# Attention output of batches 2 to 7 by plain float32 matmuls in the array's quadrants, and the tokens' scales through DRAM

## The chip, the cores and the metric

The kernel runs on one core of a Trainium2 chip. The metric is the device time of one execution in microseconds, the median of several. A core has a matrix engine (TensorE, in the profile PE for matmuls and PEld for the loads of their weights), three engines for elementwise work (VectorE or DVE, ScalarE or ACT, GpSimd or POOL), and SyncE (SP), whose queue issues all the DMAs of this kernel in program order. TensorE reads SBUF and writes PSUM, which has eight banks of 512 float32 in each of 128 partitions. Each engine does its own instructions in order and waits on semaphores for the others.

## The reference

For each of 8 batches and 8 heads, with 576 tokens and 64 features, linear attention without a softmax, a normalisation of each token within its head, and then a feed-forward layer over all 4608 tokens:

```python
kv = np.einsum('bhsd,bhse->bhde', k, v)
out = np.einsum('bhsd,bhde->bhse', q, kv)
rms = np.sqrt(np.mean(out * out, axis=-1, keepdims=True) + 1e-06)
x = out / rms * g_norm          # heads side by side: 4608 x 512
h = x @ w_in                    # 512 x 2048
y = (h / (1 + np.exp(-h))) @ w_out   # 2048 x 512
```

Everything is float32. The weights arrive as 64-bit words and are decoded in the kernel.

## The kernel before

**The feed-forward layer** is the bulk. The 4608 tokens are nine tiles of 512 (`TN`), each tile 16 steps (`NF`), one for every 128 columns of `w_in`. Operands are split into two float32r parts, upper and lower, and three products of the parts make up one product at nearly full precision. Tiles 0 and 1 are done plainly (`products`, `gate`, `project`). Tiles 2 to 4 take two steps at a time in `pair_step`, tiles 5 to 8 in `seven_step`; both use seven products for eight, and load sums of blocks of the weights from DRAM (`load_sums`, L666) twice in each pair of steps.

**The attention** of the batches that follow is threaded into these steps. `plan(b, g)` puts each piece of work of batch `b` into one of three lists, `first_jobs`, `mid_jobs` and `last_jobs`, under the number of a step; the step's code runs the lists at its beginning, in its middle and at its end. `real` maps the plan's steps to the tiles' steps, leaving out the last two of each of the tiles 0 to 4. Batches 2 to 7 start at the plan's steps 14, 23, 32, 41, 51 and 60 (`AT`), so their work lies in the tiles 0 to 5. The order is by hand (`manual_schedule`), and a tile of a pool that is full waits for the last use of the oldest one.

One batch is four pairs of heads (class `Pair`), with the features of two heads on the 128 partitions. In the order of time for batches 2 to 7:

- `load` (L266): k and v of a pair, later q, into tiles of the pool `kvq` (8 tiles), by SP.
- `kv_block` (L1240): the kv matrices of all pairs into one PSUM bank, by plain float32 matmuls in the array's left and right column halves (L277); `copy_kv` copies them on ScalarE into the two diagonal blocks of `kvm`, whose other blocks are zero.
- `split_q`, `low_q` (L299, L302) and `split_kv`, `low_kv` (L290, L293): the upper parts by ScalarE, the lower ones by VectorE. `qh` and `ql` are two more tiles of `kvq`.
- `out_half`, twice a pair: three float32r matmuls of the whole array over 256 or 320 tokens (`mm_out`, L314 to L316), then `copy_out` (L320, L321): the square and a copy out of the bank by ScalarE. The first half stands in the middle of a step, the second at its end. The banks of the attention are one PSUM bank at first and two from tile 1 on (`at_bank`).
- `turn_sq`, `sum_turned` (L325, L328): VectorE turns 32 x 32 blocks of the squares and sums them, which leaves each token's sum on the partitions of its block; four copies between partitions and `rsqrt` then make the scales by Newton steps.
- `spread` (L339): VectorE turns the scales back so that each token's scale stands on all the partitions of its head (`yT`), and `scale` (L347) multiplies `o` by it and by `g_norm`.
- `keep` (L354): SP stores the result in DRAM (`x_in_dram`), from where the later tiles load it.

The pool `tmp` has five tiles, which serve `sq`, `sqT` and `yT` here, the output rows `ob` at the end of tiles, and sums of blocks.

Of the kernel before, what the change touches and what calls it, by code (L numbers as in the profile page):

```python
# [8 lines left out]
F32 = mybir.dt.float32  # L9
# [26 lines left out]
def linear_attention_rms_silu_ffn(  # L36
# [27 lines left out]
    TN = 512  # L64
    NT = B * S // TN
    CUT = 256
    LAG = 2
    WARM = 2
    OUT7 = 5
# [184 lines left out]
    class Pair:  # L254


        def __init__(self, b, c):
            self.b, self.c = b, c
            self.kvm = kvm[c]

        def load(self, place=None, which="kvq"):


            for name in which:
                t = place() if place else kvq.tile([P, S], F32, name=name, tag="kvq")
                nc.sync.dma_start(out=t, in_={"k": k, "v": v, "q": q}[name][self.b, self.c])  # L266
                setattr(self, name, t if name == "q" else t.rearrange("p (r d) -> p r d", d=D))
# [42 lines left out]
        def mm_out(self, half):  # L310

            self.w = w = (slice(0, CUT), slice(CUT, S))[half]
            self.ps = ps = at_bank()[:, :w.stop - w.start]
            nc.tensor.matmul(out=ps, lhsT=self.kh, rhs=self.ql[:, w], start=True, stop=False)  # L314
            nc.tensor.matmul(out=ps, lhsT=self.kl, rhs=self.qh[:, w], start=False, stop=False)  # L315
            nc.tensor.matmul(out=ps, lhsT=self.kh, rhs=self.qh[:, w], start=False, stop=True)  # L316
# [27 lines left out]
        def scale(self, segment):  # L344
            a, e, t, o = (0, S, 3, 0) if segment is None else segments(self.b)[segment]
            to = x32(self.c, slice(o, o + e - a)) if t == 2 else self.o[:, a:e]
            nc.vector.scalar_tensor_tensor(  # L347
                out=to, in0=self.o[:, a:e], scalar=gcol, in1=self.yT, op0=ALU.mult, op1=ALU.mult
            )

        def keep(self):
# [4 lines left out]
        def to_tile(self, segment):  # L356
            a, e, t, o = segments(self.b)[segment]
            th, tl = (x_part(t, i, self.c)[:, o:o + e - a] for i in range(2))
            nc.scalar.copy(out=th, in_=self.o[:, a:e])
            nc.gpsimd.tensor_tensor(out=tl, in0=self.o[:, a:e], in1=th.bitcast(F32), op=ALU.subtract)  # L360

    class FirstPair(Pair):

# [101 lines left out]
    def rsqrt(sums, y, on_tensor):  # L465

        n = NP * (S // 32)
        sums, y = (t.rearrange("p c j -> p (c j)") for t in (sums, y))
        if on_tensor:
            bank = at_bank()  # L470
            m, u = bank[:, 0:n], bank[:, n:2 * n]
            nc.tensor.matmul(out=m, lhsT=both, rhs=sums, start=True, stop=True)
            calls = [lambda: nc.vector.tensor_scalar(
                out=m, in0=m, scalar1=float(D) * EPS, scalar2=None, op0=ALU.add
            )]
        else:
# [13 lines left out]
        return calls + 3 * newton(y, u, m)  # L490
# [81 lines left out]
    HF, H = NF // 2, TN // 2  # L572
    low, high = slice(0, H), slice(H, TN)
    sums_in_dram = dram.tile([HF, 2, P, 2, 2 * H], F32, name="sums_in_dram")
    out_sums = dram.tile([HF, 2, P, 2, 2 * H], F32, name="out_sums")
    operands, x_sums, once, homes, ahead = {}, {}, {}, {}, {}

# [624 lines left out]
    def at_third(n, *calls):  # L1202
        at((first_jobs, mid_jobs, last_jobs)[n % 3], n // 3, *calls)
# [12 lines left out]
    def plan(b, g):  # L1216

        ps = [Pair(b, c) for c in range(NP)]
        norms = []

        def real(g):
            if b == 1:
                return g
            if g < NF - 2:
                return g + 2
            end = OUT7 * (NF - 2)
            return g // (NF - 2) * NF + g % (NF - 2) if g < end else OUT7 * NF + 2 * (g - end)
# [12 lines left out]
        def kv_block():  # L1240

            bank = at_bank()
            for p in ps:
                p.mm_kv(bank[:, p.c * D:(p.c + 1) * D], range(4), start=p.c == 0)
            for p in ps:
                p.mm_kv(chunks=[4], stop=p.c == NP - 1)
            banks.append(bank)

        def copy_kv():

            bank = banks.pop()[:, :NP * D].rearrange("p (c d) -> p c d", d=D)
            for h in range(2):
                d = slice(h * D, (h + 1) * D)
                nc.scalar.copy(out=all_kvm[d, :, d], in_=bank[d])

        banks = []
        if b > 1:
            for p, jobs, i in zip(ps, (last_jobs, first_jobs, first_jobs, first_jobs), (-6, -5, -4, -3)):
                at(jobs, g + i, lambda p=p: p.load(which="kv"))
            at(last_jobs, g - 2, kv_block)  # L1260
            for p in ps:
                at(first_jobs, g - 1 + p.c // 3 * 2, lambda p=p: p.load(which="q"))
            at(first_jobs, g - 1, copy_kv)
        else:
            at(last_jobs, g, kv_block)
            for p in ps:
                at(first_jobs, g + 1, p.copy_kv)
        for p in ps:
            half = [lambda p=p, i=i: out_half(p, i) for i in range(2)]
            sums = lambda p=p: p.sum_sq(norms[0][:, p.c])  # L1270
            if b == 1:
                split_at, first_at, second_at, sums_at, _ = SECOND[p.c]
                at_third(split_at, p.split_kv, p.low_kv, p.split_q, p.low_q)
                at_third(first_at, p.begin_out, half[0])
                at_third(second_at, half[1])
                at_third(sums_at, *[begin] * (p.c == 0), sums)
                continue
# [7 lines left out]
            at(last_jobs, s + 3, *[begin] * (p.c == 0), lambda p=p: p.sum_turned(norms[0][:, p.c]))  # L1285
        s = g + 7
        if b == 1:
            at(chains, 12, lambda: rsqrt(*norms, True))
        else:
            calls = []  # L1290

            def some(count):
                if not calls:
                    calls.extend(rsqrt(*norms, False))
# [286 lines left out]
```

## Time and profile before

| | |
|---|---|
| Median of three runs | 804.53 us |
| The three runs | 802.23, 804.53, 806.88 us |
| Profiled execution, first to last instruction (span) | 802.5 us |
| Matmuls of `out` for batches 1 to 7 (L314 to L316), first and last start | 53 to 454 us |
| Mean granted TensorE clock | 0.997 |
| Moved by DMA | 171.08 MB, 213 GB/s |

The profile was taken of one execution. It gives its span and no separate device time. Busy times of engines are shares of the span; an engine that is not the one that sets the end may idle at no cost. A matmul's end is modelled, so the distance between starts of matmuls says what one costs, not its recorded duration. Rows of the timeline give start and duration in microseconds, engine, line, operation, what is written and read, and shape; in brackets stands the idle time of the engine before and what ended it.

### The profile page before, as it was taken

The page shows a single profiled execution, that of the slowest core. Times are in us where ns is not written, and L with a number is a line of the kernel's source. Part 1 is how long each engine was busy: PE and PEld are TensorE (multiplying, and loading weights), DVE is VectorE, ACT ScalarE, POOL GpSimd, SP SyncE. Part 2 cuts the span into 40 slices and gives each one's busy share as a digit, 9 for nine tenths or more (in the row PEclk, how much of TensorE's full clock was granted, in tenths as well). Part 3 has the DMA queues.
Part 4 walks back from the last instruction along what each step waited for, and adds up shares of the span by engine and source line. Part 5 has one row for each costly group of instructions (what it writes and reads, how often), then busy time and mean ns, then how long its engine had stood idle before and what let it go on. Part 6 is the DMA issues. An engine that isn't in the chain of part 4 may idle for free.

```text
span 802.5 us, 18480 instructions
## 1 busy us (share of the span) xinstructions
PE 788.8 (98%) x7292; PEld 782.4 (97%) x7292; DVE 611.3 (76%) x1328; ACT 413.8 (52%) x871; POOL 112.4 (14%) x116
## 2 busy tenths in 40 slices
PE   8999999999999999999999999999999999999997
PEld 7899999999999999999999999999999999999997
DVE  5999956699779678668778677678867886788666
ACT  4887555445445445535645545335644654455443
POOL 2799781332000000000000000000000000000000
PEclk9999999999999999999999999999999999999999
DMA  9994012744666856676667536986677577667653
GB/s 347 412 413 142 1 61 91 238 150 161 224 212 219 302 185 216 212 262 208 212 234 241 170 101 211 313 267 221 210 242 230 198 226 258 209 203 224 197 187 117
DMA packets 86745, 171.08 MB, mean 213 GB/s; under 512 B 8322, under 2 KB 47746, under 8 KB 86658
## 3 DMA queue, kind: packets, MB, share of 16 engines
q1 hardware_dynamic: 86658, 169.90, 62.3%
q8 instruction: 57, 0.93, 0.5%
q14 instruction: 30, 0.25, 0.1%
HBM read 137.36 MB, written 32.51 MB: 212 GB/s over the span
## 4 chain that ended last, share of the span: by engine, by line
PE 89%; DVE 3%; POOL 2%; issue 2%; ACT 2%; DMA 1%; DVEq 0%; POOLq 0%; ACTq 0%
PE hp L737 32%; PE acc L511 24%; PE acc L913 10%; PE hp L511 9%; PE at L913 5%; PE hp L913 3%; PE at L277 2%; PE at L314 1%; POOL wo L216 1%; PE at L315 1%; PE at L316 1%; DMA wi<-sums_in_dram 1%; PE hp L1340 1%; DMA out<-ob 1%; DVE x_second L729 0%
## 5 line engine op out<-in xcount | busy, mean ns | idle before, releaser
L511 PE MATMUL acc<-wo,gh 128*128 128x256 f32 x1280 | 200.8, 277 | 0.3 <-POOL wo L216 0.3
L511 PEld LDWEIGHTS acc<-wo,gh 128*128 128x128 f32 x1280 | 171.2, 188 | 0.6 <-POOL wo L216 0.5
L737 PE MATMUL hp<-x_second,wi 128*128 128x256 f32 x1152 | 154.2, 278 | 2.6 <-ACT gf L800 2.6
L737 PEld LDWEIGHTS hp<-x_second,wi 128*128 128x128 f32 x1152 | 141.9, 189 | 3.0 <-ACT gf L800 2.9
L511 PE MATMUL acc<-wo,gl 128*128 128x256 f32 x640 | 124.9, 276 | 0.0
L737 PE MATMUL hp<-operand,wi 128*128 128x256 f32 x912 | 121.1, 277 | 0.6 <-DMA wi<-sums_in_dram 0.3
L737 PEld LDWEIGHTS hp<-operand,wi 128*128 128x128 f32 x912 | 111.3, 188 | 1.2 <-DMA wi<-sums_in_dram 0.5
L511 PEld LDWEIGHTS acc<-wo,gl 128*128 128x128 f32 x640 | 96.6, 188 | 0.0
L859 ACT ACTIVATE wi<-wi 128x512 f32<-128x512 f32 x64 | 40.5, 633 | 97.7 <-DVE wi L1161 72.3
L964 POOL TENSOR_TENSOR e<-e,partial 128x256 f32<-128x256 f32 x2 | 1.5, 732 | 597.1 <-DVE e L964 597.1
L913 PE MATMUL acc<-wo,gh 128*128 128x256 f32 x256 | 46.8, 276 | 0.0
L511 PE MATMUL hp<-x_second,wi 128*128 128x256 f32 x384 | 46.3, 277 | 0.0
L511 PE MATMUL hp<-x,wi 128*128 128x256 f32 x360 | 44.5, 278 | 0.8 <-POOL x L462 0.8
L511 PEld LDWEIGHTS hp<-x_second,wi 128*128 128x128 f32 x384 | 45.0, 188 | 0.1
L511 PEld LDWEIGHTS hp<-x,wi 128*128 128x128 f32 x360 | 42.4, 188 | 1.2 <-POOL x L462 1.0
L320 ACT ACTIVATE sq<-at 128x256 f32<-128x256 f32 (+1 forms) x56 | 23.0, 411 | 39.6 <-PE at L316 31.9
L913 PE MATMUL acc<-s,gs 128*128 128x256 f32 x288 | 42.9, 276 | 0.0
L1161 DVE TENSOR_TENSOR wi<-hp,partial 128x256 f32<-128x256 f32 x32 | 13.6, 425 | 35.9 <-PE hp L737 35.9
L913 PEld LDWEIGHTS acc<-wo,gh 128*128 128x128 f32 x256 | 38.6, 188 | 0.0
L913 PEld LDWEIGHTS acc<-s,gs 128*128 128x128 f32 x288 | 37.3, 188 | 0.0
L1146 ACT COPY wi<-hp 128x256 f32<-128x256 f32 x32 | 11.9, 373 | 48.8 <-PE hp L737 48.8
L737 PE MATMUL hp<-moved,wi 128*128 128x256 f32 x288 | 36.6, 276 | 0.0
(207 smaller groups left out, 1660.1 us busy)
## 6 DMA issues: line engine op xcount, KB each, us to landing
wi<-sums_in_dram SPq DMA_DIRECT2D x112, 512.0 KB, 3.7
s<-out_sums SPq DMA_DIRECT2D x96, 256.0 KB, 4.5
wi<-in_moe_w_in SPq DMA_DIRECT2D x16, 512.0 KB, 8.1
wo<-in_moe_w_out SPq DMA_DIRECT2D x16, 512.0 KB, 9.0
sums_in_dram<-sum_parts SPq DMA_DIRECT2D x16, 512.0 KB, 2.9
out_sums<-wi SPq DMA_DIRECT2D x16, 512.0 KB, 3.0
k<-in_k SPq DMA_DIRECT2D x28, 288.0 KB, 4.6
v<-in_v SPq DMA_DIRECT2D x28, 288.0 KB, 5.1
```

Source lines behind the costliest of these rows:

```text
L216: nc.gpsimd.tensor_tensor(out=w[:, 1, :], in0=full, in1=w[:, 0, :].bitcast(F32), op=ALU.subtract)
L277: nc.tensor.matmul(out=self.kv[h], lhsT=self.k[rows, c, :], rhs=self.v[rows, c, :], start=(start and r == 0), stop=(stop and r == 4),)
L314: nc.tensor.matmul(out=ps, lhsT=self.kh, rhs=self.ql[:, w], start=True, stop=False)
L315: nc.tensor.matmul(out=ps, lhsT=self.kl, rhs=self.qh[:, w], start=False, stop=False)
L316: nc.tensor.matmul(out=ps, lhsT=self.kh, rhs=self.qh[:, w], start=False, stop=True)
L320: nc.scalar.activation(out=self.sq[:, self.w], in_=self.ps, func=AF.Square)
L511: nc.tensor.matmul(out=to[:, at:at + 256], lhsT=stationary, rhs=moving[:, at:at + 256], start=start and at == 0, stop=stop and at == n - 256,)
L737: nc.tensor.matmul(out=out, lhsT=a_of(i, a, c), rhs=x[b][:, c], start=start and n == 0, stop=n == 5, skip_group_check=not check,)
L859: nc.scalar.activation(out=self.gated, in_=self.gated, func=AF.Silu)
L913: nc.tensor.matmul(out=self.out[m], lhsT=g[m], rhs=self.weight(m, j, a), start=j == 0 and n == 0 and m in self.opens, stop=j == HF - 1 and ...
L1146: nc.scalar.copy(out=first.gated[:, low], in_=u)
L1161: nc.vector.tensor_tensor(out=first.gated[:, high], in0=u, in1=u3, op=ALU.add)
```

## The change

For batches 2 to 7:

- Four heads are one group. The host lays out q so that one tile holds, for 288 of the 576 tokens (`HS`), two heads on the upper and two on the lower 64 partitions, side by side; the heads in k and v are reordered to match. Two such tiles (`half` 0 and 1) cover a group, so a batch has four jobs (class `Job`).
- A job's `mm_out` does four plain float32 matmuls, one for each head: the stationary operand is the head's 64 x 64 kv matrix, the moving one its 64 x 288 q. A head with its features on the lower partitions and its output on the upper ones, and so on, takes each of the four quadrants. The two row halves write two PSUM banks. The upper and lower parts of q and kv, and their eight instructions per pair, are gone; kv is copied once as it is.
- The whole job, matmuls and copies out, stands at the end of a step; `turn_sq` and `sum_turned` stay where they were.
- The Newton steps stand two thirds of a step earlier. VectorE turns the scales once for the batch (`turn_scales`), SP stores them in a small buffer in DRAM (two stores), and later loads each pair's row back, repeated over the 64 partitions of each head (`load_scales`: two loads for each pair, a step ahead of `scale`). `yT` lies in `kvq`, for batch 7 in `tmp`. `scale` of batch 2 moves from the middle to the end of its step.

```diff
+    class Job:
+        def __init__(self, b, n, chunks):
+            self.b, self.n = b, n
+            self.u, self.half = divmod(n, 2)
+            self.chunks = chunks
+            self.w = slice(self.half * HS, (self.half + 1) * HS)
+
+        def load(self):
+            self.q = kvq.tile([P, S], F32, name="q", tag="kvq")
+            nc.sync.dma_start(out=self.q, in_=q[self.b, self.n])
+
+        def mm_out(self, kv):
+            self.banks = [at_bank()[:, :HS] for _ in range(2)]
+            for i, r in ((0, 0), (1, 1), (1, 0), (0, 1)):
+                rows, to = (slice(x * D, (x + 1) * D) for x in (r, i))
+                nc.tensor.matmul(
+                    out=self.banks[r][to], lhsT=kv[rows, 2 * self.u + i], rhs=self.q[rows, i * HS:(i + 1) * HS],
+                    start=True, stop=True,
+                )
+
+        def copy_out(self):
+            self.sq = tmp.tile([P, S], F32, name="sq", tag="tmp")
+            for i, (bank, chunk) in enumerate(zip(self.banks, self.chunks)):
+                if not self.half:
+                    chunk.o = opool.tile([P, S], F32, name="o")
+                nc.scalar.activation(out=self.sq[:, i * HS:(i + 1) * HS], in_=bank, func=AF.Square)
+                nc.scalar.copy(out=chunk.o[:, self.w], in_=bank)
...
         def begin():
-            norms[:] = [small.tile([P, NP, S // 32], F32, name=name) for name in ("sums", "y")]
+            sums = small.tile([P, NP, S // 32], F32, name="sums")
+            scales = small.tile([P, ROWS], F32, name="y")
+            norms[:] = sums, scales[:, :NP * (S // 32)].rearrange("p (c j) -> p c j", c=NP), scales
+            nc.gpsimd.memset(scales[:, NP * (S // 32):], 0.0)
+
+        def turn_scales():
+            turned = const.tile([P, P], F32, name="turned", tag="kh", bufs=2)[:, :ROWS]
+            nc.vector.transpose(out=turned, in_=norms[2])
+            for h in range(2):
+                nc.sync.dma_start(
+                    out=scales_in_dram[b % 2, h].rearrange("(j m) a -> m j a", m=32),
+                    in_=turned[h * D:h * D + 32].rearrange("m (j a) -> m j a", a=32),
+                )
+
+        def load_scales(p):
+            p.yT = kvq.tile([P, S], F32, name="yT", tag="kvq") if b + 1 < B else tmp.tile([P, S], F32, name="yT", tag="tmp")
+            n = S // 32
+            for h in range(2):
+                row = scales_in_dram[b % 2, h, p.c * n:(p.c + 1) * n].rearrange("(o j) a -> o (j a)", o=1)
+                nc.sync.dma_start(out=p.yT[h * D:(h + 1) * D], in_=row.to_broadcast([D, S]))
...
-            s = g + p.c
-            at(mid_jobs, s, p.split_q)
-            at(last_jobs, s, p.low_q, p.split_kv)
-            at(first_jobs, s + 1, p.low_kv)
-            at(mid_jobs, s + 2, p.begin_out, half[0])
-            at(last_jobs, s + 2, half[1])
-            at(mid_jobs, s + 3, p.turn_sq)
+            for f in fours:
+                s = g + f.n
+                at(last_jobs, s + 2, lambda f=f: f.mm_out(kv[0]), f.copy_out)
+                at(mid_jobs, s + 3, f.turn_sq)
+                at(last_jobs, s + 3, *[begin] * (f.n == 0), lambda f=f: f.sum_turned(norms[0]))
...
             for n, count in enumerate((6, 3, 3, 3)):
-                at((first_jobs, mid_jobs, last_jobs)[(2 + n) % 3], s + (2 + n) // 3, lambda count=count: some(count))
+                at((first_jobs, mid_jobs, last_jobs)[n % 3], s + n // 3, lambda count=count: some(count))
+            at(first_jobs, s + 1, turn_scales)
 
         def x_stages(p, s, *parts):
+            if b > 1:
+                at(last_jobs, s - 1, lambda: load_scales(p))
             for part in parts:
-                at(mid_jobs, s, lambda part=part: p.spread(norms[1][:, p.c], part))
-                at(mid_jobs if b <= 2 else last_jobs, s, lambda part=part: p.scale(part))
+                if b == 1:
+                    at(mid_jobs, s, lambda part=part: p.spread(norms[1][:, p.c], part))
+                at(mid_jobs if b == 1 else last_jobs, s, lambda part=part: p.scale(part))
             if b > 1:
                 at(first_jobs, s + 1, p.keep)
```

More of the change, by code (lines that the diff above doesn't have):

```diff
@@ L347, in scale @@
             nc.vector.scalar_tensor_tensor(
-                out=to, in0=self.o[:, a:e], scalar=gcol, in1=self.yT, op0=ALU.mult, op1=ALU.mult
+                out=to, in0=self.o[:, a:e], scalar=gcol, in1=self.yT[:, a:e] if self.b > 1 else self.yT,
+                op0=ALU.mult, op1=ALU.mult,
             )
@@ L360, in to_tile, with turn_sq, sum_turned @@
             nc.gpsimd.tensor_tensor(out=tl, in0=self.o[:, a:e], in1=th.bitcast(F32), op=ALU.subtract)
+    class Job:
[22 more added lines that the diff above has]
+                nc.scalar.copy(out=chunk.o[:, self.w], in_=bank)
+        def turn_sq(self):
+            self.sqT = tmp.tile([P, S], F32, name="sqT", tag="tmp")
+            nc.vector.transpose(out=self.sqT, in_=self.sq)
+        def sum_turned(self, sums):
+            blocks = HS // 32
+            nc.vector.tensor_reduce(
+                out=sums[:, 2 * self.u:2 * self.u + 2, self.half * blocks:(self.half + 1) * blocks],
+                in_=self.sqT.rearrange("p (c j a) -> p c j a", c=2, a=32), axis=AX.X, op=ALU.add,
+            )
     class FirstPair(Pair):
@@ L574, in linear_attention_rms_silu_ffn @@
     sums_in_dram = dram.tile([HF, 2, P, 2, 2 * H], F32, name="sums_in_dram")
+    scales_in_dram = dram.tile([2, 2, ROWS, 32], F32, name="scales_in_dram")
     out_sums = dram.tile([HF, 2, P, 2, 2 * H], F32, name="out_sums")
@@ L1249, in copy_kv @@
         def copy_kv():
[L1251 to L1256, printed above, removed]
+            kv.append(const.tile([P, NP, D], F32, name="kv_all", tag="kvm"))
+            nc.scalar.copy(out=kv[0], in_=banks.pop()[:, :NP * D].rearrange("p (c d) -> p c d", d=D))
+        banks, kv = [], []
         if b > 1:
+            fours = [Job(b, n, ps[n // 2 * 2:n // 2 * 2 + 2]) for n in range(NP)]
             for p, jobs, i in zip(ps, (last_jobs, first_jobs, first_jobs, first_jobs), (-6, -5, -4, -3)):
@@ L1260, in plan @@
             at(last_jobs, g - 2, kv_block)
-            for p in ps:
-                at(first_jobs, g - 1 + p.c // 3 * 2, lambda p=p: p.load(which="q"))
+            for f in fours:
+                at(first_jobs, g - 1 + f.n // 3 * 2, f.load)
             at(first_jobs, g - 1, copy_kv)
+            for f in fours:
+                s = g + f.n
+                at(last_jobs, s + 2, lambda f=f: f.mm_out(kv[0]), f.copy_out)
+                at(mid_jobs, s + 3, f.turn_sq)
+                at(last_jobs, s + 3, *[begin] * (f.n == 0), lambda f=f: f.sum_turned(norms[0]))
         else:
@@ L1267, in plan @@
                 at(first_jobs, g + 1, p.copy_kv)
-        for p in ps:
+        for p in ps if b == 1 else ():
             half = [lambda p=p, i=i: out_half(p, i) for i in range(2)]
             sums = lambda p=p: p.sum_sq(norms[0][:, p.c])
[L1271 to L1277, printed above, removed]
-            s = g + p.c
-            at(mid_jobs, s, p.split_q)
-            at(last_jobs, s, p.low_q, p.split_kv)
-            at(first_jobs, s + 1, p.low_kv)
-            at(mid_jobs, s + 2, p.begin_out, half[0])
-            at(last_jobs, s + 2, half[1])
-            at(mid_jobs, s + 3, p.turn_sq)
-            at(last_jobs, s + 3, *[begin] * (p.c == 0), lambda p=p: p.sum_turned(norms[0][:, p.c]))
+            split_at, first_at, second_at, sums_at, _ = SECOND[p.c]
+            at_third(split_at, p.split_kv, p.low_kv, p.split_q, p.low_q)
+            at_third(first_at, p.begin_out, half[0])
+            at_third(second_at, half[1])
+            at_third(sums_at, *[begin] * (p.c == 0), sums)
         s = g + 7
         if b == 1:
-            at(chains, 12, lambda: rsqrt(*norms, True))
+            at(chains, 12, lambda: rsqrt(*norms[:2], True))
         else:
@@ L1293, in some @@
                 if not calls:
-                    calls.extend(rsqrt(*norms, False))
+                    calls.extend(rsqrt(*norms[:2], False))
                 for _ in range(count):
@@ L1554, in lay_out @@
             b, h, s, d = a.shape
-            a = a.transpose(0, 1, 3, 2).reshape(b, h // 2, 2 * d, s)
+            a = a.transpose(0, 1, 3, 2)
+            fours = a[2:].reshape(b - 2, h // 4, 2, 2, d, 2, s // 2).transpose(0, 1, 5, 2, 4, 3, 6)
+            pairs, fours = a[:2].reshape(2, h // 2, 2 * d, s), fours.reshape(b - 2, h // 2, 2 * d, s)
+            a = np.concatenate([pairs, fours])
         elif name in ("k", "v"):
             b, h, s, d = a.shape
-            a = a.reshape(b, h // 2, 2, s, d)
+            fours = a[2:].reshape(b - 2, h // 4, 2, 2, s, d).transpose(0, 1, 3, 2, 4, 5).reshape(b - 2, h, s, d)
+            a = np.concatenate([a[:2], fours]).reshape(b, h // 2, 2, s, d)
             whole = a[:, :, :, :512].reshape(b, h // 2, 8, 128, d).transpose(0, 1, 3, 2, 4)
```

3 lines of the change are left out of this document (added).

## The prediction

> **What bounds the kernel now.** I read the page's busy shares first, then windows of 20 us along the span.
>
> ```profile
> span 802.5 us, 18480 instructions
> ...
> PE 788.8 (98%) x7292; PEld 782.4 (97%) x7292; DVE 611.3 (76%) x1328; ACT 413.8 (52%) x871; POOL 112.4 (14%) x116
> ```
>
> ```profile
> 240.00:260.00 20.00, 20.00 (x178) 20.00 (x176) 18.77 (x37) 11.29 (x26) 0.00 (x0) 1.00 0.67 215
> 220.00:240.00 20.00, 19.79 (x228) 19.30 (x227) 14.37 (x40) 9.58 (x19) 0.00 (x0) 1.00 0.64 218
> 320.00:340.00 20.00, 17.62 (x139) 17.62 (x140) 13.60 (x28) 10.63 (x25) 0.00 (x0) 0.91 0.62 213
> 500.00:520.00 20.00, 19.68 (x174) 19.48 (x173) 14.32 (x34) 9.23 (x19) 0.00 (x0) 1.00 0.91 308
> ```
>
> TensorE is busy in 98% of the span. The windows give, for each stretch, the busy time and number of instructions of PE, PEld, DVE, ACT and POOL, then the granted clock, the DMA share and GB/s. A window without a stall holds 178 matmuls in 20 us, one every 0.112 us. So only two things can move the time: TensorE's own work, and its stalls. Between 60 and 780 us one stall matters: the window 320 to 340 holds 139 matmuls, 39 too few, and 39 x 0.112 = 4.4 us. The timeline shows its cause:
>
> ```profile
> 319.28 0.78 DVE L339 STREAM_TRANSPOSE yT<-y 128x576 f32<-128x576 f32 x1 [1.39 <-DMA out<-ob]
> ...
> 320.83 0.38 ACT L320 ACTIVATE sq<-at 128x256 f32<-128x256 f32 x1 [4.54 <-DVE sqT L325]
> ...
> 322.38 2.51 PE L737 MATMUL hp<-x_second,wi 128*128 128x256 f32 x12 [2.60 <-ACT gf L800]
> ```
>
> The five `tmp` tiles were full. VectorE's yT waited 1.39 us for the store of `ob` to land. Behind it sqT was late, and ScalarE's next sq (a half of `out` put in the middle of a step) needed the tile that sqT reads, so it idled 4.54 us with the copy of L800 (`gf`) queued behind it. TensorE needed L800's copy, idled 2.60 us, and then ran the next matmuls slowly: 12 in 2.51 us, where 12 at 0.112 take 1.35. The granted clock of that window is 0.91.
>
> **TensorE, removed.** One pair of heads of batches 2 to 7 now takes two halves, of 256 and of 320 columns. The second:
>
> ```profile
> 312.25 0.30 PE L314 MATMUL at<-ql,kh 128*128 128x320 f32 x1
> 312.39 0.31 PE L315 MATMUL at<-qh,kl 128*128 128x320 f32 x1
> 312.53 0.31 PE L316 MATMUL at<-qh,kh 128*128 128x320 f32 x1
> 312.68 0.28 PE L511 MATMUL acc<-wo,gh 128*128 128x256 f32 x1
> ```
>
> From start to start 0.43 us; the first half is three matmuls of the usual width, 3 x 0.112 = 0.33; together 0.76 us. Six batches of four pairs: 24 x 0.76 = 18.2 us go.
>
> **TensorE, added.** In their place stand 24 jobs of four plain float32 matmuls, each 64 rows by 64 columns with 288 moving columns. The trace has plain float32 matmuls in column halves, from Rest.make_out (L406), between full-array neighbours:
>
> ```profile
> 22.39 0.27 PE L390 MATMUL acc<-ident,on 128*128 128x128 f32 x1
> 22.59 0.32 PE L406 MATMUL at<-kvm,early_wo 128*64 128x128 f32 x1
> 22.59 0.32 PE L406 MATMUL at<-kvm,early_wi 128*64 128x128 f32 x1
> 22.75 0.27 PE L406 MATMUL at<-kvm,early_wo 128*64 128x128 f32 x1
> 22.75 0.27 PE L406 MATMUL at<-kvm,early_wi 128*64 128x128 f32 x1
> 22.86 0.27 PE L406 MATMUL at<-kvm,early_wo 128*64 128x128 f32 x1
> 22.86 0.27 PE L406 MATMUL at<-kvm,early_wi 128*64 128x128 f32 x1
> 22.97 0.27 PE L406 MATMUL at<-kvm,early_wo 128*64 128x128 f32 x1
> 22.97 0.27 PE L406 MATMUL at<-kvm,early_wi 128*64 128x128 f32 x1
> 23.18 0.39 PE L511 MATMUL acc<-x,wi 128*128 128x256 f32 x1
> ```
>
> Four calls left eight records: a plain float32 matmul is two passes. A pass of 128 columns takes 0.11 us (22.86 to 22.97), and the two column halves run it at the same time. By columns, a pass of 288 takes 0.11 x 288/128 = 0.25 us. The rows also price the change of shape. Going in: L390 is through at 22.39 + 0.11 = 22.50, the first pass really begins one pass before the second, at 22.75 - 0.11 = 22.64, so 0.14. Coming out: the last pass is through at 23.08, L511 starts at 23.18 and is recorded with 0.39 instead of the usual 0.28, so 0.10 + 0.11 = 0.21. Together 0.35 us for each job, which the old full-array halves did not pay.
>
> The Trainium skill, "TensorEngine Tiling (Array Packing)", section Key Properties, says that a change of tiling mode drains TensorE. That speaks against this change and the 0.35 us agrees; the page has no figure.
>
> What no row shows is two row halves that share columns. Both kinds of splitting at once, but on the diagonal (64*64), end each kv block:
>
> ```profile
> 227.75 2.63 PE at L277 x80
> 230.37 1.58 PE hp L737 x12
> 231.96 1.36 PE acc L511 x12
> ```
>
> 2.63 us and the 0.22 that the next dozen lost are 2.85; less three changes of shape at 0.17 leaves 2.34 for 40 simultaneous pairs, 0.058 each for 64 columns, near 0.11/2. So diagonal quadrants do run together. The bounds for one job: four at once 0.35 + 0.02 (later starts) + 2 x 0.25 = **0.87 us**; two at once 0.35 + 4 x 0.25 = 1.35; one after the other 0.35 + 8 x 0.25 = 2.35. I take 0.87: where two calls use different parts of the array, every row shows them overlapping, and each call of a job has a quadrant and its own bank half. 24 x (0.87 - 0.76) = **+2.6 us**.
>
> **ScalarE and VectorE.** Gone are, for each of 24 pairs, these (yT 20 times whole, and in pieces for batch 2), and two smaller ones of 128 columns (kh, kl) that I leave out of the sum:
>
> ```profile
> L302 DVE TENSOR_TENSOR ql<-q,qh 128x576 fp32r<-128x576 f32 x28 | 22.4, 801 | 0.0
> ...
> L299 ACT CAST qh<-q 128x576 fp32r<-128x576 f32 x28 | 19.2, 685 | 0.0
> ...
> L339 DVE STREAM_TRANSPOSE yT<-y 128x576 f32<-128x576 f32 x20 | 15.4, 769 | 1.4 <-DMA out<-ob 1.4
> ```
>
> VectorE loses 24 x (0.80 + 0.77) = 38 us and gains six turns of 128x96 (under 0.77 each). ScalarE loses 24 x 0.685 = 16 us and half of its twelve kv copies; the two squares and two copies of a pair stay, over 288 columns. In the time this is worth nothing by itself, since both had slack in the full windows (18.8 and 11.3 of 20 us). It counts only at the stall.
>
> **The stall.** yT leaves `tmp` (batch 7 excepted) and VectorE, and a job's squares move to the end of the step, behind the L800 copy. The `ob` tiles and the sums' tiles stay, so sqT now meets the full pool where yT did and still waits until about 319.2. Then VectorE's next read of the products' bank follows one transpose instead of two, 0.78 us sooner, and L800 stands in front of the job's squares instead of behind them. Of the 2.60 us of idling I keep 0.6, and no slow clock: **-3.8 us**, between -4.4 (gone) and 0 (unchanged).
>
> **The scales' way.** Per batch: one turn, two stores of 12 KB, then four times two loads of 144 KB that repeat a row for 64 partitions. All ten issues go to SP, which is in order and also carries the loads of sums.
>
> ```profile
> L666 SPq DMA_DIRECT2D wi<-sums_in_dram x55: 319/326/1537, 217.1 to 519.7; - x55
> ...
>   PE hp L737: 0.3, 1
> ```
>
> ```profile
> q<-in_q SPq DMA_DIRECT2D x28, 288.0 KB, 3.7
> ...
> x_in_dram<-o SPq DMA_DIRECT2D x4, 32.0 KB, 5.0
> ```
>
> The first fence is the view of L666 from 215 to 520 us (least, median and most ns of an issue; below, who waited for it): an issue costs 0.33 us, so ten cost 3.3 us per batch, spread over five steps, and TensorE waited for a load of sums once, 0.3 us. The second has the microseconds from issue to landing last. If an issue slips in ahead of a load of sums, that comes 0.7 us later at most. New waits: the first load waits for the store's landing (nearest row: 5.0 us for 32 KB), and behind it on SP stand `keep` and the next load of sums, due about half a pair of steps later. `scale` on VectorE waits for its load (288 KB in 3.7 us; two of 144 KB), issued one step before. A pair of steps is 90 matmuls, 10.1 us, so one step is 5 us: the loads land in time, barely. The first pair of a batch has 5.0 + 3.7 = 8.7 us for 1.67 steps, 8.4 us. Behind a late `scale` VectorE holds the adds that TensorE's products wait for, some 24 matmuls (2.7 us) later, which hides a wait of one or two us. Bounds: nothing, or two stalls like the old one, 8.8 us. I take **+0.4**. The 7 MB more of traffic stand beside 171 MB, and a window without a stall has a DMA share of 0.67. The loads of k, v and q keep their places; all eight kvq tiles are again held at most just before a kv block.
>
> **Sum.** +2.6 - 3.8 + 0.4 = -0.8: the profiled span of 802.5 becomes 801.7. It lies 2.0 below the median of the runs shown (804.53, of 802.23 to 806.88); carried over to the median this gives **803.7 us**. A measurement of this kernel can tell about 0.5% (4 us) from no change.
>
> **The rivals.**
>
> *Two quadrants at a time* (slower). If the two row halves of the same columns take turns, a job costs 1.35 instead of 0.87: 24 x 0.48 = +11.5, 815.2 us. For it: no row shows that overlap. Against it: every other pair of parts overlaps. It decides from about 1.07 us per job on: 24 x 0.20 = 4.8 turns the -0.8 into 4 above. Chance 0.14.
>
> *Strict order of the passes.* If a second pass held back the next call, a job would need five passes one behind the other, 0.35 + 5 x 0.25 = 1.60, and the time would be 803.7 + 24 x 0.73 = 821.2 us. The rows of L406 speak against it: its calls are c = 0 (early_wo), then c = 1 (early_wi), and the passes start wo, wi, wo, wi. Chance 0.03. (The Trainium skill, "TensorE: Matmul & The Clock Gate", section The mechanism in Part 3, has matmuls start and end strictly in program order; the L406 rows do not agree.)
>
> *The wait moves.* Four at once, but the stall stays (+3.8, 807.5), or a late load of scales makes one more of its size (+4.4, 811.9). For it: the margins above are under a microsecond. Against it: VectorE is some 36 us freer. About 808; chance 0.22.
>
> *More goes.* The idle 0.21 and 0.32 us of the windows at 220 and 500 vanish too, the stall goes whole, no new wait comes, and the change of shape costs a sixth less (0.06 of 0.35) for the smaller quadrants: 804.5 + 2.6 - 1.4 - 4.4 - 0.5 = 800.8 us. For it: VectorE and ScalarE have less to do. Against it: nothing in the rows prices a quadrant's change lower. Chance 0.07.
>
> **How the numbers follow.** The forecast has 0.54, with a range of its own of 801 to 806. Eight in ten: 800.5 to 815.5 takes in all but the strict order and tails on both sides. Faster by over 0.5% (below 800.5): 0.04 from the forecast's tail and 0.04 of the last rival, 0.08. Slower (above 808.5): 0.14 + 0.03, half of the moved wait, 0.01 of the forecast: 0.29. Within: 0.63.
>
> **What would show it.** In the changed profile a job's eight records should start in two groups of four, 0.25 us apart; two groups of two more mean the first rival. From the last full-array matmul before a job to the first after it should lie 0.87 us beyond their own time. The window about 320 should hold some 170 matmuls at clock 1.00. VectorE's row of `scale` should wait under 1 us for DMA; a wait of 3 us there, followed by an idle TensorE, is the moved wait. The prediction is wrong if a job costs over 1 us, or TensorE idles over 2 us in total between 160 and 520 us.

## The result and the profile after

| | median of runs | lowest to highest | span of the profiled execution |
|---|---|---|---|
| Kernel before | 804.14 us (4 runs) | 802.23 to 806.88 | 802.5 us |
| Changed kernel | 833.61 us (4 runs) | 832.39 to 833.88 | 832.0 us |

The ratio is 1.0351 [1.0333, 1.0369]: the change makes the kernel 3.5% slower. The forecast was 803.7 us with a range of 800.5 to 815.5, so the prediction was wrong, by 30 us and outside its range.

Line numbers have moved: L511 of before is L558 now, L737 is L785, L913 is L961 (in some of the runs below they are one less). `hp` is written by the products with `w_in`, `acc` by those with `w_out`. First the page's span and busy shares:

```profile
span 832.0 us, 18509 instructions
...
PE 820.7 (99%) x7340; PEld 801.0 (96%) x7340; DVE 580.0 (70%) x1258; ACT 394.4 (47%) x817; POOL 112.2 (13%) x123
```

VectorE and ScalarE do less, as foreseen (the splitting of q and kv that is gone was four instructions a pair, two on each of them, not the eight that the description of the change has). TensorE is busy for 820.7 us instead of 788.8 and idle for 11.3 instead of 13.7. So the time didn't come from waiting. The windows of the changed kernel (busy time and number of instructions of PE, PEld, DVE, ACT and POOL, then clock, DMA share, GB/s) say the same:

```profile
240.00:260.00 20.00, 20.00 (x170) 20.00 (x170) 11.41 (x23) 7.06 (x13) 0.00 (x0) 1.00 0.81 266
320.00:340.00 20.00, 20.00 (x174) 18.29 (x173) 14.14 (x27) 11.04 (x26) 0.00 (x0) 1.00 0.77 249
500.00:520.00 20.00, 20.00 (x170) 19.96 (x170) 12.60 (x27) 9.81 (x20) 0.00 (x0) 1.00 0.81 266
600.00:700.00 100.00, 100.00 (x846) 100.00 (x845) 73.51 (x181) 47.14 (x95) 0.00 (x0) 1.00 0.67 219
```

The stall at 320 us is gone, the granted clock is 1.00, none of these four windows idles, and yet a window without a stall holds 170 matmuls where it held 178. The last row matters most: it lies behind all of the changed work, and the same stretch of before holds 39 matmuls more in 100 us (113 ns each against 118):

```profile
600.00:700.00 100.00, 100.00 (x885) 100.00 (x884) 77.59 (x191) 49.36 (x100) 0.00 (x0) 1.00 0.69 222
```

The loss begins ahead of the changed work, too. These are the first products with `gh`, in the tokens' tile 0, 100 us before the first job of the new kind; first the changed kernel, then before (start, duration, and in the last column how many matmuls the row covers):

```profile
32.32 0.64 PE L558 MATMUL acc<-wo,gh 128*128 128x256 f32 x4
32.80 0.40 PE L558 MATMUL acc<-wo,gl 128*128 128x256 f32 x2
33.04 0.64 PE L558 MATMUL acc<-wo,gh 128*128 128x256 f32 x4
...
34.72 2.99 PE L558 MATMUL hp<-x,wi 128*128 128x256 f32 x24
37.55 0.40 PE L558 MATMUL acc<-wo,gh 128*128 128x256 f32 x2
```

```profile
31.31 0.62 PE L511 MATMUL acc<-wo,gh 128*128 128x256 f32 x4
31.76 0.39 PE L511 MATMUL acc<-wo,gl 128*128 128x256 f32 x2
31.99 0.62 PE L511 MATMUL acc<-wo,gh 128*128 128x256 f32 x4
...
33.57 2.88 PE L511 MATMUL hp<-x,wi 128*128 128x256 f32 x24
36.29 0.39 PE L511 MATMUL acc<-wo,gh 128*128 128x256 f32 x2
```

Six matmuls of acc take 0.72 us instead of 0.68 (32.32 to 33.04, 31.31 to 31.99), that is 120 ns each instead of 113; the 24 of hp take 2.83 instead of 2.72, 118 ns instead of 113. From the starts of all records of full-array matmuls with 256 columns, pauses left out, the mean distance is 118.5 ns against 113.5; there are about 6,400 of them, and 6,400 x 5.0 ns = 32 us. The time grew by 29.5. So the slower matmuls account for the whole loss, and a part of it comes back because TensorE idles less (2.4 us by the busy times above).

Some of the slowness is passed on. In the changed kernel the hp products right behind matmuls of another shape (a kv block, a job) still go at the old pace: of the 24 behind the job at 136.12 us, all but the first few start 113 to 114 ns apart. The acc products behind them go at 120, and from there on the hp products go at 118, up to the next such break.

**Where the place in SBUF comes in.** Nothing in the code of these matmuls changed. In the compiled programs one thing about their operands did: the address of `gh` and `gl` (and in the later tiles of `gs`, which lies partly in the same places). SBUF tiles get their addresses pool behind pool, the same byte offsets in each partition. The change lets the scales' tile `y` of the pool `small` grow from 288 to 384 bytes (96 columns, for the turn), times two buffers 192 bytes, and the pool behind `small` is `gp`, with `gh`, `gl` and `gf`. The kernel before has lines that do nothing but push a pool along, and that the part ahead of the prediction didn't mention:

```python
    gap(const, 128, "gap_first")
    gap(kvq, 192, "gap_q")
    gap(gp, 64, "gap_gated")
    gap(const, 96, "gap_x")
```

Places of the first byte, modulo 256 (`gh` and `gl` are the stationary operand of the acc products and `wo` the moving one; `wi` and `x` are the same for hp):

| | gh, gl | wo | wi | x |
|---|---|---|---|---|
| before (gp at byte 214784) | 0 | 192 | 0 | 192 |
| changed (gp at byte 214976) | 192 | 192 | 0 | 192 |

### The profile page after: what moved, and what is told of

Same layout as the page of the kernel before. It is cut to its first block, busy times and chain, and to the rows that moved or that the text cites. A ratio compares the mean times of both kernels' runs of the same rounds, so it can differ in the third digit from the quotient of the medians.

```text
span 832.0 us, 18509 instructions
## 1 busy us (share of the span) xinstructions
PE 820.7 (99%) x7340; PEld 801.0 (96%) x7340; DVE 580.0 (70%) x1258; ACT 394.4 (47%) x817; POOL 112.2 (13%) x123
## 4 chain that ended last, share of the span: by engine, by line
PE 96%; DVE 1%; DMA 1%; issue 1%; ACT 0%; POOL 0%; SPq 0%; DVEq 0%; ACTq 0%; POOLq 0%
PE hp L785 33%; PE acc L558 27%; PE acc L961 11%; PE hp L558 10%; PE at L961 6%; PE hp L961 3%; PE at L279 2%; PE at L385 2%; PE hp L1407 1%; DMA wi<-sums_in_dram 1%; PE acc L424 0%; PE hp L279 0%; DVE ob L1012 0%; DVE on L488 0%; PE at L316 0%
## 5 line engine op out<-in xcount | busy, mean ns | idle before, releaser
L558 PE MATMUL acc<-wo,gh 128*128 128x256 f32 x1280 | 209.4, 284 | 0.0
L558 PEld LDWEIGHTS acc<-wo,gh 128*128 128x128 f32 x1280 | 177.4, 192 | 3.8 <-issue 3.5
L785 PE MATMUL hp<-x_second,wi 128*128 128x256 f32 x1152 | 159.0, 282 | 0.0
L785 PEld LDWEIGHTS hp<-x_second,wi 128*128 128x128 f32 x1152 | 145.0, 189 | 4.1 <-issue 3.9
L558 PE MATMUL acc<-wo,gl 128*128 128x256 f32 x640 | 128.6, 283 | 0.0
L785 PE MATMUL hp<-operand,wi 128*128 128x256 f32 x912 | 125.0, 281 | 1.0 <-DMA wi<-sums_in_dram 0.6
L785 PEld LDWEIGHTS hp<-operand,wi 128*128 128x128 f32 x912 | 114.9, 189 | 1.4 <-issue 0.8
L558 PEld LDWEIGHTS acc<-wo,gl 128*128 128x128 f32 x640 | 99.8, 192 | 0.0
L961 PE MATMUL acc<-wo,gh 128*128 128x256 f32 x256 | 48.8, 283 | 0.0
L558 PEld LDWEIGHTS hp<-x_second,wi 128*128 128x128 f32 x384 | 45.7, 188 | 3.1 <-issue 3.1
L558 PE MATMUL hp<-x_second,wi 128*128 128x256 f32 x384 | 48.0, 281 | 0.0
L558 PE MATMUL hp<-x,wi 128*128 128x256 f32 x360 | 45.5, 281 | 0.8 <-POOL x L509 0.8
L558 PEld LDWEIGHTS hp<-x,wi 128*128 128x128 f32 x360 | 43.4, 189 | 1.2 <-POOL x L509 1.0
L961 PE MATMUL acc<-s,gs 128*128 128x256 f32 x288 | 44.3, 282 | 0.0
L961 PEld LDWEIGHTS acc<-wo,gh 128*128 128x128 f32 x256 | 39.9, 192 | 0.0
L961 PEld LDWEIGHTS acc<-s,gs 128*128 128x128 f32 x288 | 38.6, 190 | 0.0
L785 PE MATMUL hp<-moved,wi 128*128 128x256 f32 x288 | 37.9, 281 | 0.0
L577 ACT ACTIVATE gh<-hp 128x512 fp32r<-128x512 f32 x31 | 18.4, 595 | 40.0 <-PE hp L558 39.9
L579 DVE TENSOR_TENSOR gl<-gf,gh 128x512 fp32r<-128x512 f32 x18 | 13.0, 725 | 35.0 <-ACT gf L578 31.6
```

The lines of the kernel that those rows point to most:

```text
L558: nc.tensor.matmul(out=to[:, at:at + 256], lhsT=stationary, rhs=moving[:, at:at + 256], start=start and at == 0, stop=stop and at == n - 256,)
L577: nc.scalar.activation(out=gh, in_=hp[:, :TN], func=AF.Silu)
L579: (nc.gpsimd if t == 0 and f >= WARM else nc.vector).tensor_tensor(out=gl, in0=gf, in1=gh.bitcast(F32), op=ALU.subtract)
L785: nc.tensor.matmul(out=out, lhsT=a_of(i, a, c), rhs=x[b][:, c], start=start and n == 0, stop=n == 5, skip_group_check=not check,)
L961: nc.tensor.matmul(out=self.out[m], lhsT=g[m], rhs=self.weight(m, j, a), start=j == 0 and n == 0 and m in self.opens, stop=j == HF - 1 and ...
```

## The experiments

Theory A: the 192 bytes by which `gp` moved make the loss, and the quadrants and the scales' way do what was predicted. Rivals: the quadrants leave TensorE slower for what follows; the traffic through DRAM disturbs it. Each run stands beside runs of the kernel before on the same chip, whose times lay between 803.2 and 819.7 with medians of 806.58, 805.70 and 805.13 in the three sets.

### The change with gp at a good place, and before at the bad one

The changed kernel with the pool `gp` made ahead of `small`, which puts it at byte 212992, 0 mod 256:

```diff
-    small = ctx.enter_context(tc.tile_pool(name="small", bufs=2))
     gp = ctx.enter_context(tc.tile_pool(name="gp", bufs=LAG + 1))
+    small = ctx.enter_context(tc.tile_pool(name="small", bufs=2))
```

> The changed kernel with one thing more changed: the pool gp (gh, gl, gf) is made ahead of the pool small, so that gh and gl begin at 212992 and not at 214976 bytes of a partition: 0 and not 192 modulo 256, as before the change (214784). Theory A (placement: the scales' larger tiles pushed gp by 192 bytes, and gh and gl as stationary operands now lie as wo, the moving one, does, which slows TensorE's full-array matmuls): cadence of the 256-column matmuls back from 118-120 to 113 ns, time 803.7 us as forecast, 802 to 808. Rival B (the quadrant matmuls or the DMA traffic slow TensorE for good): 831 to 835 us, cadence 118-120 ns.

Measured: 805.64 us (12 runs), ratio to before 1.0004 [0.9972, 1.0035]. The products run at 113 ns again. The window that held 846 in the changed kernel, in this run:

```profile
600.00:700.00 100.00, 100.00 (x885) 100.00 (x884) 77.58 (x191) 49.44 (x100) 0.00 (x0) 1.00 0.68 221
```

The other way round, the kernel before with 192 bytes more in front of `gp`:

```diff
-    gap(gp, 64, "gap_gated")
+    gap(gp, 256, "gap_gated")
```

> The kernel before, with nothing of the change but gp 192 bytes further on (a gap of 256 in place of 64 bytes), so that gh and gl have the very addresses that they have after the change. Theory A: cadence 118-120 ns from the first product with wo on, some 6300 matmuls x 5 ns = +31 us, 830 to 840 us. Rival B: 804 us, 113 ns.

Measured: 834.08 us (4 runs), ratio 1.0339 [1.0291, 1.0387]. The same window:

```profile
600.00:700.00 100.00, 100.00 (x846) 100.00 (x845) 73.28 (x180) 46.97 (x95) 0.00 (x0) 1.00 0.67 217
```

The same 846, with nothing of the change in the kernel. That settles theory A: 192 bytes of padding alone cost what the change cost, and without them the change costs nothing that can be told from zero. The rivals fall.

### The quadrants alone

The changed kernel, with the scales spread by VectorE as before (`spread`, no DRAM). The tile `y` is then small again, so `gp` is back at byte 214784.

```diff
-            at(first_jobs, s + 1, turn_scales)
...
-            if b > 1:
-                at(last_jobs, s - 1, lambda: load_scales(p))
             for part in parts:
-                if b == 1:
-                    at(mid_jobs, s, lambda part=part: p.spread(norms[1][:, p.c], part))
+                at(mid_jobs, s, lambda part=part: p.spread(norms[1][:, p.c], part))
```

> The changed kernel with the quadrant matmuls and the new layout of the heads, but the scales spread by VectorE as before (no DRAM, small tiles of the old size, so gp stays at 214784). Theory A: 113 ns; jobs +2.6 us, the stall at 320 us partly gone: 803 to 808 us. Rival B in the form that the quadrants slow TensorE: 831 to 835 us; in the form that the DMAs of scales do: 803 to 808.

Measured: median 807.33 us (12 runs), ratio 0.9996 [0.9949, 1.0043], but the twelve times lie in two heaps, 801.07 to 802.80 and 811.85 to 812.84. The profiled execution is of the lower heap: span 799.5, no stall above 0.4 us, 113 ns.

### What counts about the place

First everything behind `gap_x` (x, weights, the attention's tiles, gp) 64 bytes further, so that no distance between these operands changes:

```diff
-    gap(const, 96, "gap_x")
+    gap(const, 160, "gap_x")
```

> The kernel before with gap_x 64 bytes larger: x, the weights, kvq, tmp, opool, small and gp all move by 64 bytes together, so the distances between stationary and moving operands stay what they were. Theory A with the distance between the two operands as what counts: 802 to 807 us, 113 ns. Theory A with the place of the stationary operand alone as what counts (gh at 64 and wi at 64 modulo 256): slower, 815 to 840 us.

Measured: 811.07 us (806.11 to 818.95, 10 runs), ratio 1.0054 [1.0006, 1.0102]. Neither as good as before nor as bad as the changed kernel. The profiled execution (span 815.8) has both paces in one program:

```profile
300.00:320.00 20.00, 20.00 (x177) 20.00 (x177) 16.84 (x33) 11.31 (x25) 0.00 (x0) 1.00 0.57 189
600.00:620.00 20.00, 20.00 (x172) 20.00 (x171) 12.31 (x32) 7.93 (x16) 0.00 (x0) 1.00 0.73 242
```

From 280 to 310 us its products run at 113 to 114 ns, from 491 to 800 us all at 118, and from there to the end mostly at 113 again. Up to 490 us the pace goes back and forth between 113 and 118, for acc and hp alike. It changes at a break in the row of products (halves of `out`, a kv block, a short wait) and then holds to the next: of some 70 stretches of more than eight products between such breaks, all but two keep one pace from their first few products on. The last break before the long slow stretch is a wait of 0.2 us at 490:

```profile
487.59 1.52 PE L737 MATMUL hp<-operand,wi 128*128 128x256 f32 x12
488.95 0.62 PE L511 MATMUL acc<-wo,gh 128*128 128x256 f32 x4
...
490.09 0.39 PE L511 MATMUL acc<-wo,gl 128*128 128x256 f32 x2
490.52 0.97 PE L737 MATMUL hp<-operand,wi 128*128 128x256 f32 x6
...
493.45 1.58 PE L737 MATMUL hp<-x_second,wi 128*128 128x256 f32 x12
494.86 0.40 PE L511 MATMUL acc<-wo,gh 128*128 128x256 f32 x2
```

Twelve hp products take 1.36 us ahead of it (487.59 to 488.95) and 1.41 behind it (493.45 to 494.86). So the pace isn't a plain function of the distance between the operands; at one and the same placement it can be either, and it keeps what it has until something breaks the row.

Then single shifts in the kernel before: `gp` by 64 and by 128 bytes, `wo` by 64 (the 64 bytes of `gap_weights` ahead of wo's blocks instead of behind them), and both `gp` by 192 and `wo` by 64.

```diff
-    gap(gp, 64, "gap_gated")
+    gap(gp, 128, "gap_gated")
```

> The kernel before, with gap_gated 128 instead of 64: gh, gl and gf begin 64 bytes further in each partition, at 64 mod 256; nothing else moves. Theory C (what counts is the place modulo 128, so that 64 is as bad as the 192 of the run e2): start to start of acc<-wo,gh about 120 ns, of hp about 118, time 834. Theory D (what counts is that gh lies at the same place modulo 256 as wo, which lies at 192): 113 ns, time 803 to 808.

```diff
-    gap(gp, 64, "gap_gated")
+    gap(gp, 192, "gap_gated")
```

> The kernel before, with gap_gated 192 instead of 64: gh, gl and gf begin 128 bytes further, at 128 mod 256; nothing else moves. Both theories: 113 ns, time 803 to 808 (modulo 128 it is the place of before, and it is not the place of wo modulo 256). 118 to 120 ns and over 820 would mean that only 0 mod 256 is good.

```diff
         for kind in ("wo", "wi"):
+            if kind == "wo":
+                gap(weights, 64, "gap_weights")
             for f in range(NF):
                 block(kind, f, F32)
-            if kind == "wo":
-                gap(weights, 64, "gap_weights")
```

> The kernel before, with the 64 bytes of gap_weights ahead of the blocks of wo instead of behind them: wo begins at 0 mod 256 like gh, which now lies at the same place as what it is multiplied with; nothing else moves. Theory A2 (the place of the stationary gh decides, alone): 113 ns, time 803 to 808. Theory B2 (the distance between the stationary and the moving operand decides): acc<-wo,gh 118 to 120 ns, and over 825.

The fourth is the last edit together with `gap(gp, 256, "gap_gated")`:

> The kernel before, with gh, gl and gf at 192 mod 256 as in the changed kernel, and wo at 0 mod 256: their distance modulo 128 is that of before, with the two sides exchanged. Theory A2 (the place of gh alone): 120 ns, time about 834 as in the run e2. Theory B2 (the distance): 113 ns, time 803 to 815.

Measured, with the number of matmuls from 600 to 700 us of each run:

| gh, gl / wo, mod 256 | run | median us (runs) | matmuls, 600 to 700 us |
|---|---|---|---|
| 0 / 192 | before (in the first profile) | 805.70 (10) | 885 |
| 128 / 192 | e6 | 804.89 (8) | 885 |
| 64 / 192 | e5 | 820.79 (2) | 860 |
| 0 / 0 | e7 | 820.99 (2) | 870 |
| 192 / 0 | e8 | 821.48 (2) | 860 |
| 192 / 192 | e2 | 834.08 (4) | 846 |

The rows of e7 and e6, one at a bad place and one at a good one:

```profile
600.00:700.00 100.00, 100.00 (x870) 100.00 (x869) 72.46 (x180) 47.44 (x96) 0.00 (x0) 1.00 0.70 227
```

```profile
600.00:700.00 100.00, 100.00 (x885) 100.00 (x884) 77.66 (x190) 49.21 (x99) 0.00 (x0) 1.00 0.68 223
```

Of six placements two keep 113 ns in their profiles. Run e6 came out as both theories had it. The other three answered neither: e5 is not as bad as 192 (against "modulo 128 only"), e7 is slow though gh did not move (against "gh's place alone"), e8 is slow though the distance modulo 128 is that of before (against "the distance alone"). What holds is that the places of both operands matter, `wo` by itself (e7) as well as `gh` by itself (e2, e5). Runs e5, e7 and e8 have two times each, so their intervals are wide (e7: 1.0152 [0.9964, 1.034]), but their profiles show the slower pace directly. A rule that gives all six rows was not found.

The Trainium skill, "SBUF — State Buffer", section "SBUF: two separate sides", has contention on the engines' side only at the pair of ports that VectorE and GpSimd share, and says that PE's own ports wait on nobody. That names no effect of where an operand starts on TensorE's pace; runs e2 and e7 show one, with 846 and 870 matmuls in the stretch where before has 885. The Trainium skill, "SBUF — State Buffer", section "Specifications (TRN2)", names cachelines of 16 bytes with a penalty for each crossing to a new one; all the shifts of this study are multiples of 64 bytes and leave the crossings as they are, so that does not explain the rows either.

### Better places for the changed kernels

Since 128 was good, three runs use it: the quadrants alone, the changed kernel (by leaving out the line `gap_gated`), and that one with the scales' stores issued later. The quadrants alone:

```diff
-    gap(gp, 64, "gap_gated")
+    gap(gp, 192, "gap_gated")
```

> The run e3 (quadrants kept, scales spread by VectorE as before) with gap_gated 192: gh, gl and gf at 128 mod 256, as in the run e6, whose eight times lay between 803.39 and 807.34 where before's ten lay between 803.64 and 819.73. If the two heaps of e3 (801 and 812) come from TensorE slipping into the slower pace, and the place at 128 keeps it out of it: all times 800.5 to 804, and faster than before by 0.4 to 0.8 per cent. If the heaps have another cause: again about half of the times at 812.

Measured: 801.42 us, all twelve runs between 800.73 and 802.49, ratio 0.9922 [0.9886, 0.9958]. One heap instead of two, and the fastest kernel of the study. The 0.8% of the ratio has two parts: seven of the 25 times of before that it compares with lie above 810 us, and none of e9's. Against the other eighteen (median 804.4) e9 is 2.9 us or 0.4% faster, as it is by the spans (798.9 against 802.5). Its page:

```profile
span 798.9 us, 18450 instructions
...
PE 788.0 (99%) x7340; PEld 768.7 (96%) x7340; DVE 591.4 (74%) x1280; ACT 393.1 (49%) x817; POOL 112.5 (14%) x116
```

The changed kernel:

```diff
-    gap(gp, 64, "gap_gated")
```

> The changed kernel without its line gap_gated: gh, gl and gf at 128 mod 256, nothing else moved. By the map of e2, e5 and e6 (0 and 128 good, 64 and 192 bad): 113 ns, 803 to 807, that is the changed kernel without its loss. If the change itself slowed TensorE, 118 to 120 ns and over 820.

Measured: 805.56 us (802.71 to 807.26, 10 runs), ratio 0.9959 [0.9917, 1.0000]. One line less takes the whole loss away. What is left between this run and e9, 4.1 us by the medians and 803.0 against 798.9 by the spans, is the price of the scales' way through DRAM; `gp` lies at the same place in both (0.5 us of the spans' difference is there at 100 us already, ahead of the changed work). One stall makes up nearly half of it. First the waits of PE and of SP (engine, line waited for, total, times, longest), then SP's issues:

```profile
PE hp L784 <- DMA wi<-sums_in_dram: 2.0, 2, 1.7
```

```profile
SPq L1291 <- DVE turned L1289: 6.1, 1, 6.1
```

```profile
288.07 0.79 SPq L1291 DMA_DIRECT2D scales_in_dram<-turned  x2
288.95 1.33 SPq L378 DMA_DIRECT2D q<-in_q  x3
290.37 0.38 SPq L713 DMA_DIRECT2D wi<-sums_in_dram  x1
290.85 1.11 SPq L1302 DMA_DIRECT2D yT<-scales_in_dram  x2
```

SP stands 6.1 us for VectorE's turn. Behind it wait three loads of q and the load of sums, which then are issued together with the loads of the scales. In the run e9 the same load of sums goes out at 287.22 us, 3.15 earlier. TensorE is 1.4 us further on there in e9, so the load is some 1.8 us later in e10 for the work that needs it. The DMA view of the stretch from 286 to 298 us of run e10 (KB of each, median microseconds to landing) shows the crowd:

```profile
wi<-sums_in_dram SPq DMA_DIRECT2D x2, 512.0 KB, 7.2
q<-in_q SPq DMA_DIRECT2D x3, 288.0 KB, 3.2
yT<-scales_in_dram SPq DMA_DIRECT2D x4, 144.0 KB, 7.2
```

A load of sums lands in 4.0 us over the whole of run e10; here in 7.2. So TensorE waited 1.7 us.

The last edit puts the two stores behind the step's load of sums:

```diff
             nc.vector.transpose(out=turned, in_=norms[2])
+            norms.append(turned)
+
+        def store_scales():
+            turned = norms.pop()
             for h in range(2):
...
             at(first_jobs, s + 1, turn_scales)
+            at(last_jobs, s + 1, store_scales)
```

> The run e10 with the two stores of the scales issued at the end of their step (last_jobs) instead of with the transpose at its start, behind the step's load of sums on SP. If SP's wait of 6.1 us for the turned scales at 288 us, with the loads of sums behind it, makes TensorE's stall of 1.58 us at 295: that wait is under 2 us, the stall is gone, and the kernel is 1 to 2.5 us faster than e10. If the stall has another cause: within 0.7 us of e10.

Measured: 807.07 us (805.69 to 809.1, 10 runs), 1.5 us slower than e10 where 1 to 2.5 us faster was expected. Half of the expectation held: SP's wait for the turn and the stall at 295 us are gone. The other half failed, because the loads of the scales are late in their place:

```profile
PE hp L784 <- DVE gf L857: 3.5, 2, 2.3
PE hp L784 <- DMA wi<-sums_in_dram: 0.5, 1, 0.5
```

```profile
245.00 0.82 DVE L348 SCALAR_TENSOR_TENSOR o<-o,gcol,yT 128x576 f32<-128x576 f32 x1 [4.08 <-DMA yT<-scales_in_dram]
...
246.34 0.42 DVE L857 TENSOR_TENSOR gf<-hp,wi 128x256 f32<-128x256 f32 x1
```

VectorE waits 4.08 us for the scales, the add of L857 comes behind, and TensorE idles 2.27 us at 246.81 for that. The wait moved from one engine's queue to another's. Each of the two orders that were tried makes somebody late.

For a look at the upper heap of run e3, its kernel ran once more:

> The kernel of the run e3 once more, for a profile, whose twelve times fell into two heaps at 801 and 812. If the heaps are two paces of TensorE: a profile with about 801 shows 113 ns throughout, one with about 812 a long stretch at 117 to 118 ns, worth some 10 us. If not: 113 ns in both, and a stall of 11 us somewhere.

Measured: 801.75 us, 113 ns throughout. It fell into the lower heap, so this run told nothing about the upper one.

## Why the prediction was wrong

**The step that failed** is in the first part: "A window without a stall holds 178 matmuls in 20 us, one every 0.112 us. So only two things can move the time: TensorE's own work, and its stalls." The work was counted in instructions, and the 0.112 us was taken for a constant of the kernel. It depends on where the operands lie, and, as e4 shows, at one placement also on what went before. The change moved the pool behind a tile that grew by 96 bytes, and 6,400 matmuls went from 113.5 to 118.5 ns. The size of `y` and the `gap` lines stood in the diff and in the kernel; asking what the latter are for might have shown the risk. Both signs of being wrong that the prediction set itself stayed off in the changed kernel (a job costs 0.85 us, TensorE idles 0.95 us between 160 and 520): they looked at the jobs and at the stalls, and the loss lay in the other products.

The other steps, by the runs at good places:

- **Removed.** 0.76 us a pair was forecast. Counted from the matmul before to the third behind, less their 113 ns each, the halves cost 0.34 and 0.45 us: 0.79.
- **Added.** 0.87 us a job was forecast. By the same count a job costs 0.85 us in the run e9. The four quadrants run at once, which was the assumption without a row. Sum of both steps, unrounded: 24 x (0.854 - 0.788) = +1.6 instead of +2.6. A job of the changed kernel, eight records of which four start at 136.12 to 136.14 and four at 136.41 to 136.43 us (0.29 apart; forecast 0.25):

```profile
135.79 0.40 PE L558 MATMUL acc<-wo,gl 128*128 128x256 f32 x2
136.12 0.72 PE L385 MATMUL at<-q,kv_all 64*64 64x288 f32 x8
136.76 3.01 PE L558 MATMUL hp<-x_second,wi 128*128 128x256 f32 x24
```

- **The stall.** -3.8 us was forecast. Place for place along the program, run e3 is 1.3 us behind before at 316 us and 3.2 us ahead of it at 327: -4.4 us, the whole of it. Some 1.6 us of that are the slow matmuls behind the stall (12 in 2.51 us), and those don't always come: in the run e6, the kernel before with `gp` elsewhere, the stall is there with 2.57 us, but the 12 matmuls behind it take 1.48 us and the window's granted clock is 1.00.
- **The scales' way.** +0.4 us was forecast, 4.1 were measured (e10 against e9), within the bounds of 0 to 8.8. The sentence that fell is "If an issue slips in ahead of a load of sums, that comes 0.7 us later at most": the store in front didn't take its 0.8 us of issuing, but SP's wait of 6.1 us for the turn. An issue of a scales' load took 0.59 us (median), not 0.33. `scale` waited up to 3.62 us for its load in the run e10, not under 1, and what stood behind it on VectorE hid that there, as forecast, though not in e11.
- **The sum** without the pace: +1.6 - 4.4 + 4.1 = +1.3, 803.8 as a span; e10 had 803.0 and e1 802.5. So the forecast's time would have stood had `gp` stayed in its place, though partly by luck: the scales' way cost 3.7 us more than forecast, the jobs and the stall 1.6 less.

**The rivals.** Neither the two that would have slowed TensorE (two quadrants at a time, strict order) nor the others name the cause. The times they gave, 815 and 821, lie in the right direction for a reason that the 0.85 us refutes. "The wait moves" came true in the runs e10 (a late load of sums) and e11 (late loads of the scales), at a few microseconds. The sign "the window about 320 should hold some 170 matmuls at clock 1.00" was met (174), but not for its reason: at 113 ns it would have held 180, as e1's does.

Against e1, which is the same kernel with `gp` at its old place modulo 256, TensorE is busy 31.5 us longer in the changed kernel (820.7 against 789.2) and idle 2.0 us less (11.3 against 13.3). That makes the 29.5 us between their spans. The waits for loads of sums went from 1.6 to 0.6 us; that a slower TensorE gives the loads more time fits this, but was not tried by itself.

**What stays open.** Why the operands' places change the pace, and by which rule. That the upper heap of e3, and before's times above 810, are executions that slipped into the slower pace fits e4's profile, and also that with `gp` at 128 none of forty executions (e6, e9, e10, e11) took over 810 us, where 21 of the 68 of before did; but no profile of such an execution was taken.

## What to carry over

A change that alters the size of any tile moves the pools behind it: where TensorE is the bound, compare the addresses of the matmuls' operands before and after, and count the matmuls of a window far from the change; if that count differs, look at the places before the change's logic. Lines that only pad are part of the tuning, and a change of one is tried alone. A queue in order charges a new entry for what it waits for, not for its time of issue, and a wait that is moved has to be priced again where it goes.

## What was not expected of the hardware

- The same full-array matmul of 256 columns is issued every 113 or every 117 to 120 ns, at granted clock 1.00, depending on shifts of 64 to 192 bytes in the operands' offsets. The recorded time of a matmul's weight load changes with it (last figure before the second bar, mean ns; the changed kernel, then before):

```profile
L558 PEld LDWEIGHTS acc<-wo,gh 128*128 128x128 f32 x1280 | 177.4, 192 | 3.8 <-issue 3.5
```

```profile
L511 PEld LDWEIGHTS acc<-wo,gh 128*128 128x128 f32 x1280 | 171.2, 188 | 0.6 <-POOL wo L216 0.5
```

- The pace is sticky. In the changed kernel products whose own operands did not move (`hp`, stationary `wi`, moving `x`) run at 118 ns behind slow ones, and at 113 behind a kv block or a job. In e4 a break can switch the pace either way: a wait of 0.2 us at 490 us took it from 113 to 118, where it stayed to 800 us.
- Four plain float32 matmuls of 64 x 64 in the four quadrants, each in two passes over 288 columns, cost 0.85 us together with both changes of shape.
